# GeGLU feed-forward on one core: one plain feature tile instead of two, sixteen P2 tiles ahead instead of ten, and a new order of loads at the start

## The chip, the cores and the metric

The kernel runs on one core of one Trainium2 chip (trn2). The metric is the device time of one execution in microseconds (us). Executions of one kernel mostly agree within 0.3%, so differences of less than 1% have to be read with care here: every ratio below is that of a kernel to the kernel before, run in alternation with it on the same chip, and it comes with a 95% interval. Times in the text that begin "at 29.2 us" count from the start of the profiled span.

## The reference

```python
B, S, D, F = 32, 32, 1024, 3584          # 1024 tokens, bf16 throughout
def reference(x, w_gate, w_up, w_down):
    return (gelu_tanh(x @ w_gate) * (x @ w_up)) @ w_down
```

## The kernel before

The two projections x @ w_gate and x @ w_up are computed together, one 128-column feature tile at a time (28 tiles). For a tile, gate and up are the two block rows of a 2x2 block matrix A, the two halves of D are its block columns; x, transposed, is a 2x2 block matrix B of D halves by token halves. A plain product of the two costs 8 block products of 4 matmuls, 32 matmuls of 128x128 by 128x512. Twenty-six of the tiles are done with seven block products (Strassen-Winograd) instead, 28 matmuls: P1 = A11 B11, P2 = A12 B21, S1 T1, S2 T2, S3 T3, S4 B22 and A22 T4. P1 and P2 take bf16 operands as they come from memory; S1 to S4 (sums of weight blocks) and T1 to T4 (sums of x blocks) are made on chip in fp32r, a 4-byte type that the profile prints as f32 at the matmuls. Those tiles go in pairs ("chunks"). DVE makes the four T and the sums of the first pair, POOL makes the sums of all later pairs.

Products are summed up in banks of PSUM, the memory that PE writes; psA, psB and psC in the profile are such banks.

The first tiles are plain, because plain products need nothing but bf16 loads. Some P2 products also need only loads; they are made at the start and kept in fp32 ("ahead"), in groups of four tiles. So plain tiles and P2 groups are what TensorE (PE) does while x, the weights and the T matrices are still being prepared.

```python
FC = 2                       # tiles in a chunk
NAHEAD = 10                  # P2 tiles made ahead
KB = 4                       # P2 tiles in a group
...
# start of the queue of loads (SP); load_xT is a DMA transpose of x
load_ahead(0, 0, 1); ...                        # gate rows of group 0
load_xT(0, KD + KQ, DT)                         # rest of B21
load_ahead(0, KQ, KD)
load_w0(nc.sync, KD + KQ, DT)                   # weights of the plain tiles
load_ahead(1, 0, KD)
load_xT(0, 0, KD)                               # B11
load_w0(nc.sync, 0, KD)
load_xT(1, 0, KD)                               # B12
load_xT(1, KD, DT)                              # B22
... later: load_w_all(1, 1); load_w_all(1, 0)   # weights of the first pair
           load_ahead(2, 0, KD); load_w_all(2, 0)
...
# end of the start
tt(t2, b22, t1, SUB)
nc.scalar.copy(b22r, b22)
chunk1 = sums(1, nc.vector)                     # first pair's sums, on DVE
for _ in range(3):
    next(chunk1)
...
p1 = [acc("A") for _ in range(FC)]
for fl in range(FC):
    prod(p1[fl], quads(1, fl)[0], b11, True)    # P1 of the first pair
...
begun = [first_product(FC + fl, p1[fl]) for fl in range(FC)]   # adds ahead + P1 on DVE
tt(t3, b22, b12, SUB)
next(chunk1)
tt(t4, b21, t2, SUB)
nc.gpsimd.tensor_copy(ident[:, :1], t4[:, 0, :1])   # POOL starts only when T4 is there
...
for ci in range(1, NCH):                        # the pairs
    ... sums(ci + 1, nc.gpsimd)                 # next pair's sums, on POOL
    for fl in range(FC):
        prod(psc[fl], s1[fl], t1, True)
    for fl in range(FC):
        prod(psa[fl], s2[fl], t2, False)        # onto P1's bank: after DVE's add has read it
    for st in open_fts:
        last_product(st)                        # A22 T4 of the pair before
    ... S4 B22; P2, unless it was made ahead; P1 of the next pair; S3 T3
```

The down projection (w_down) follows as one more seven-product scheme; the change does not touch it.

Of the kernel before, what the change touches and what calls it, by code (L numbers as in the profile page):

```python
# [13 lines left out]
def kernel(  # L14
# [37 lines left out]
    NCH = FT // FC  # L52
    NAHEAD = 10
# [21 lines left out]

    def g_tiles(name, dtype, cols):

        return [
            gpool.tile(
                [P, k1 - k0, cols],  # L80
                dtype,
                name=name,
                tag=f"{name[:2]}{k1 - k0}",
                bufs=2,
            )
            for k0, k1 in batches
        ]

    g_lo = g_tiles("lo", bf16, N)
# [8 lines left out]
    def g_of(ft):  # L98
        k = ft % HF
        return by_batch(g_lo if ft < HF else g_hi)(k)  # L100
# [15 lines left out]
    def x_rows(dt, nb):  # L116
        return ((b11, b12), (b21, b22))[dt // KD][nb][:, dt % KD, :]


    ahead = [  # L120
        gpool.tile([P, n, NB], fp32, name="ahead", tag=f"hi{n}", bufs=2) for n in (KB, KB, QF - KB)
    ]
    assert 2 * KB < NAHEAD <= KB + QF
# [7 lines left out]
    def load_w(eng, ci, which, d0, d1):  # L131
        f0 = ci * FC * P
        src = (wg_r, wu_r)[which]
        eng.dma_start(out=w_tiles[ci, which][:, d0:d1, :], in_=src[:, d0:d1, f0 : f0 + FC * P])

    def load_w_all(ci, which):

        alloc_w(ci, which)
        if ci < NCH - 2:
            load_w(nc.sync, ci, which, 0, KD if which == 0 and is_ahead(ci) else DT)  # L140
            return


        for d0 in (0, KD):
            load_w(nc.sync, ci, which, d0, d0 + KD)

    def is_ahead(ci):
        return 0 < ci and (ci + 1) * FC <= FC + NAHEAD

    def quads(ci, fl=None):  # L150
        cols = slice(None) if fl is None else slice(fl * P, (fl + 1) * P)
        wg, wu = w_tiles[ci, 0], w_tiles[ci, 1]
        a12 = wg[:, KD:, cols]
        if is_ahead(ci):
            i, j = divmod((ci - 1) * FC, KB)
            a12 = a12_ahead[i][:, :, j * P : (j + FC) * P][:, :, cols]
# [4 lines left out]
    def sums(ci, eng):  # L161
# [3 lines left out]
            spool.tile([P, KD, FC * P], f32r, name=n, tag=n) for n in ("s1", "s2", "s4", "s3")  # L165
# [6 lines left out]

    a22rs = {}

    def a22r_of(ft):
        t = spool.tile([P, KD, P], f32r, name="a22r", tag="a22r", bufs=2)
        nc.scalar.copy(t, quads(*divmod(ft, FC))[3])
# [11 lines left out]
    with tc.manual_schedule():  # L189
# [12 lines left out]
        def load_ahead(i, k0, k1, eng=nc.sync):  # L202
            f0, n = FC + i * KB, min(KB, NAHEAD - i * KB)
            eng.dma_start(
                out=a12_ahead[i][:, k0:k1, : n * P],
                in_=wg_r[:, KD + k0 : KD + k1, f0 * P : (f0 + n) * P],
            )
# [14 lines left out]
        for which, eng in enumerate((nc.sync, nc.scalar)):  # L222
            load_w(eng, 0, which, KD, KD + KQ)
        load_xT(0, KD + KQ, DT)
# [4 lines left out]
        load_w0(nc.sync, 0, KD)  # L229
        load_xT(1, 0, KD)  # L230
        load_xT(1, KD, DT)

# [17 lines left out]
        def plain(ps, which, fl, nb, d0, d1, first=0, last=DT - 1):  # L250
            for dt in range(d0, d1):
                nc.tensor.matmul(  # L252
                    ps,
                    lhsT=w_tiles[0, which][:, dt, fl * P : (fl + 1) * P],
# [10 lines left out]
        def plain_out(ft, nb, h, up):  # L265
            tt(g_of(ft)[:, nb * NB : (nb + 1) * NB], h, up, MUL)
# [12 lines left out]
        def ahead_of(ft):  # L279
            i, j = divmod(ft - FC, KB)  # L280
            return ahead[i][:, j, :]

# [10 lines left out]


        ps = [acc(t) for t in "CCAA"]

        def plain0(tok0, d0, d1):
            for which in (0, 1):
                for dt in range(d0, d1):
                    for fl in range(FC):  # L300
                        plain(tok0[fl][which], which, fl, 0, dt, dt + 1, KD, KD - 1)
# [9 lines left out]
        tok0 = [(acc("A"), acc("B")) for _ in range(FC)]  # L311
        plain0(tok0, KD, KD + KQ)
        for j, copy in enumerate((nc.scalar.copy, nc.vector.tensor_copy) * 2):
            product_ahead(ps[j], 0, j, KQ)
            copy(ahead[0][:, j, :], ps[j])
        plain0(tok0, KD + KQ, DT)
        a12_ahead.append(xpool.tile([P, KD, (NAHEAD - 2 * KB) * P], bf16, name="a12b"))
        load_w_all(1, 1)
        load_w_all(1, 0)
        load_ahead(2, 0, KD)  # L320
        load_w_all(2, 0)
        for j, tag in enumerate("CCAA"):
            ps = acc(tag)
            product_ahead(ps, 1, j)
            (nc.scalar.copy, nc.vector.tensor_copy)[j % 2](ahead[1][:, j, :], ps)
        for fl in range(FC):
            for which in (0, 1):
                plain(tok0[fl][which], which, fl, 0, 0, KD, KD, KD - 1)
            plain_out(fl, 0, gelu(tok0[fl][0], "h0", 4), tok0[fl][1])
            if fl == 0:  # L330
                tt(t1, b12, b11, SUB)
        tok1 = [(acc("A"), acc("B")) for _ in range(FC)]
        for fl in range(FC):
            for which in (0, 1):
                plain(tok1[fl][which], which, fl, 1, 0, KD)
        tt(t2, b22, t1, SUB)
        nc.scalar.copy(b22r, b22)
# [3 lines left out]
        for fl in range(FC):  # L341
            for which in (0, 1):
                plain(tok1[fl][which], which, fl, 1, KD, DT)
            tok1[fl] = gelu(tok1[fl][0], "h0", 4), tok1[fl][1]
        load_w_all(2, 1)

# [11 lines left out]
        def first_product(ft, psa=None):  # L358
            if psa is None:
                psa = acc("A")  # L360
                prod(psa, quads(*divmod(ft, FC))[0], b11, True)
            if ft < FC + NAHEAD:
                return psa, gelu(added(ahead_of(ft), psa), "h0", 4)
# [252 lines left out]
```

## Time and profile before

| | before |
|---|---|
| time, median of 5 | 275.05 us (274.71 to 275.57) |
| profiled span | 273.3 us |
| PE busy | 267.9 us, 98% |
| first fp32r product (S1 T1 of the first pair) | at 29.18 us |
| S1 T1 of the second pair | at 38.36 us |
| a pair without / with its own P2 | 10.84 / 12.56 us |

The page's first part shows busy time, share of the span and number of instructions of each engine:

```profile
PE 267.9 (98%) x1190; PEld 188.9 (69%) x1206; DVE 196.6 (72%) x196; ACT 110.8 (41%) x181; POOL 108.3 (40%) x55
```

The list of waits, for PE alone (who waited, for what; us in total, times, longest), says that PE practically never waits:

```profile
PE psA L235 <- PEq L600: 0.8, 1, 0.8
PE psC L285 <- DMA a12a<-in_w_gate_dram: 0.5, 1, 0.5
```

PE's timeline around the first pair (start, duration, engine, line, operation; a merged row counts its matmuls, and its duration runs to the modelled end of the last one):

```profile
27.48 1.89 PE L285 MATMUL psC<-b,a12b 128*128 128x512 bf16 x8
29.18 2.12 PE L270 MATMUL psC<-t,s 128*128 128x512 f32 x8
31.13 2.00 PE L270 MATMUL psA<-t,s 128*128 128x512 f32 x8
32.97 1.98 PE L270 MATMUL psC<-b22r,s 128*128 128x512 f32 x8
36.33 2.19 PE L270 MATMUL psA<-t,s 128*128 128x512 f32 x8
38.36 1.98 PE L270 MATMUL psC<-t,s 128*128 128x512 f32 x8
```

Rows follow each other without a gap. From the starts of such rows, eight bf16 matmuls take 1.73 us (216 ns each) and eight fp32r ones 1.815 us (227 ns). The Trainium skill, "TensorE: Matmul & The Clock Gate", section Back-to-back issue gap, gives 512/2.4 + 2.5, about 216 ns, for the isolated spacing of matmuls with 512 columns; the bf16 rows agree with it, and the fp32r rows take 5% more.

DVE's timeline over the same stretch (first sum of the first pair, the two adds on P1's banks, T3, T4):

```profile
23.00 1.22 DVE L168 TENSOR_TENSOR s<-wu 128x1024 fp32r<-128x1024 bf16 x1
26.81 0.69 DVE L350 TENSOR_TENSOR c<-ahead,psA 128x512 f32<-128x512 f32 x1
27.68 0.69 DVE L350 TENSOR_TENSOR c<-ahead,psA 128x512 f32<-128x512 f32 x1 [0.17 <-PE psA L270]
28.28 2.28 DVE L379 TENSOR_TENSOR t<-b,b 128x2048 fp32r<-128x2048 bf16 x1
31.62 2.29 DVE L381 TENSOR_TENSOR t<-b,t 128x2048 fp32r<-128x2048 bf16 x1
```

The adds end at 28.4 us, and PE wants to accumulate S2 T2 onto those banks only at 31.13 us. T4 ends at 33.9 us; POOL then makes the second pair's S1, ready at 36.4 us, 1.9 us before PE wants it at 38.36. So DVE is busy, and has slack.

### The profile page before, as it was taken

The numbers are of one execution on the slowest core, as the hardware profiler recorded it, in microseconds if no ns is written. First come the engines' busy times: TensorE is split into PE (matmuls) and PEld (weight loads), VectorE is DVE, ScalarE is ACT, GpSimd is POOL, SyncE is SP. The second block draws the span as 40 slices with busy tenths as digits, with TensorE's granted clock in tenths as the row PEclk, the third lists the DMA queues.
The fourth block names the chain that finished last, engine by engine and source line by source line (L and its number), as shares of the span: only waits on it lengthen the run. The fifth ranks groups of instructions, "written<-read, shape, count | busy, mean of one in ns | idle before, by whom it ended". The sixth has DMA issues, their size and how long they took to land.

```text
span 273.3 us, 3350 instructions
## 1 busy us (share of the span) xinstructions
PE 267.9 (98%) x1190; PEld 188.9 (69%) x1206; DVE 196.6 (72%) x196; ACT 110.8 (41%) x181; POOL 108.3 (40%) x55
## 2 busy tenths in 40 slices
PE   8999999999999999999999999999999999999995
PEld 4444777877778676676868686754447888888883
DVE  1269996877756676776667576568999999999611
ACT  1271664554643646455563636430300032972001
POOL 1000099997897694949576684000000000000000
PEclk9999999999999999999999999999999999999999
DMA  7994321414505405050514280004992254786202
GB/s 166 290 251 105 111 75 40 117 42 113 156 11 143 137 19 155 0 153 0 156 28 126 79 269 1 0 2 132 329 342 83 93 175 163 240 279 203 78 0 78
DMA packets 53841, 33.77 MB, mean 124 GB/s; under 512 B 9792, under 2 KB 53824, under 8 KB 53824
## 3 DMA queue, kind: packets, MB, share of 16 engines
q1 hardware_dynamic: 50304, 31.00, 39.3%
q10 hardware_dynamic: 3520, 2.56, 2.9%
q8 instruction: 9, 0.15, 0.3%
q14 instruction: 8, 0.07, 0.1%
HBM read 29.62 MB, written 2.10 MB: 116 GB/s over the span
## 4 chain that ended last, share of the span: by engine, by line
PE 97%; DMA 1%; issue 0%; ACT 0%; SPq 0%
PE psA L270 34%; PE psA L446 18%; PE psC L270 17%; PE psC L446 7%; PE psB L446 7%; PE psB L270 5%; PE psB L252 3%; PE psA L252 2%; PE psC L285 2%; PE psA L285 1%; DMA a12a<-in_w_gate_dram 1%; ACT o_sb L586 0%; SPq L191 0%; PE tp L243 0%
## 5 line engine op out<-in xcount | busy, mean ns | idle before, releaser
L270 PE MATMUL psA<-t,s 128*128 128x512 f32 x208 | 54.2, 402 | 0.0
L262 ACT ACTIVATE h<-c 128x512 bf16<-128x512 f32 x52 | 31.6, 627 | 36.6 <-DVE c L350 36.6
L270 PEld LDWEIGHTS psA<-t,s 128*128 128x128 f32 x208 | 39.1, 188 | 9.2
L168 POOL TENSOR_TENSOR s<-wu 128x1024 fp32r<-128x1024 bf16 x12 | 27.4, 2285 | 23.7 <-PE psC L270 12.8
L350 DVE TENSOR_TENSOR c<-sn,psA 128x512 f32<-128x512 f32 x26 | 17.8, 684 | 16.8 <-PE psA L270 16.8
L270 PEld LDWEIGHTS <-wg 128*128 128x128 bf16 x168 | 15.4, 98 | 20.1 <-issue 3.4
L169 POOL TENSOR_TENSOR s<-s,wg 128x1024 fp32r<-128x1024 f32 x12 | 27.7, 2312 | 0.9
L171 POOL TENSOR_TENSOR s<-wg,wu 128x1024 fp32r<-128x1024 bf16 x12 | 26.6, 2216 | 0.0
L355 ACT COPY sn<-psA 128x512 f32<-128x512 f32 x42 | 23.6, 584 | 6.8 <-PE psA L270 6.8
L355 ACT COPY sn<-psC 128x512 f32<-128x512 f32 x26 | 15.2, 588 | 26.9 <-PE psC L270 22.8
L270 PE MATMUL psA<-t,a22r 128*128 128x512 f32 x104 | 25.9, 391 | 0.0
L270 PE MATMUL psC<-t,s 128*128 128x512 f32 x104 | 25.8, 390 | 0.0
L270 PE MATMUL psC<-b22r,s 128*128 128x512 f32 x104 | 25.7, 389 | 0.0
L270 PE MATMUL psA<-b,wg 128*128 128x512 bf16 x100 | 24.1, 379 | 0.2
L270 PEld LDWEIGHTS psC<-t,s 128*128 128x128 f32 x104 | 19.4, 188 | 4.4 <-ACT ahead L377 0.3
L270 PEld LDWEIGHTS psA<-t,a22r 128*128 128x128 f32 x104 | 19.5, 188 | 4.1
L270 PEld LDWEIGHTS psC<-b22r,s 128*128 128x128 f32 x104 | 19.5, 188 | 4.1
L350 DVE TENSOR_TENSOR c<-sn,psC 128x512 f32<-128x512 f32 x26 | 17.7, 688 | 5.5 <-PE psC L270 5.5
L369 DVE TENSOR_TENSOR hi<-h,psA 128x512 bf16<-128x512 bf16 x14 | 9.6, 689 | 12.5 <-PE psA L270 12.5
L425 DVE TENSOR_TENSOR hi<-c,h 128x512 bf16<-128x512 f32 x14 | 18.0, 1284 | 0.5
L425 DVE TENSOR_TENSOR lo<-c,h 128x512 bf16<-128x512 f32 x12 | 17.8, 1479 | 0.6
L170 POOL TENSOR_TENSOR s<-wg,s 128x1024 fp32r<-128x1024 bf16 x8 | 17.3, 2156 | 0.6
(94 smaller groups left out, 396.9 us busy)
## 6 DMA issues: line engine op xcount, KB each, us to landing
wdb<-in_w_down_dram SPq DMA_DIRECT2D x12, 512.0 KB, 5.0
wu<-in_w_up_dram SPq DMA_DIRECT2D x11, 512.0 KB, 4.0
wdb<-in_w_down_dram SPq DMA_DIRECT2D x12, 384.0 KB, 4.7
wg<-in_w_gate_dram SPq DMA_DIRECT2D x6, 512.0 KB, 5.1
wg<-in_w_gate_dram SPq DMA_DIRECT2D x10, 256.0 KB, 4.4
v<-in_w_down_dram SPq DMA_DIRECT2D x4, 512.0 KB, 6.7
out_dram<-o_sb ACTq DMA_DIRECT2D x16, 128.0 KB, 1.7
v<-in_w_down_dram SPq DMA_DIRECT2D x4, 384.0 KB, 7.6
```

The lines of the kernel that those rows point to most:

```text
L168: yield eng.tensor_tensor(s1, a21, a22, ADD)
L169: yield eng.tensor_tensor(s2, s1, a11, SUB)
L170: yield eng.tensor_tensor(s4, a12, s2, SUB)
L171: yield eng.tensor_tensor(s3, a11, a21, SUB)
L252: nc.tensor.matmul(ps, lhsT=w_tiles[0, which][:, dt, fl * P : (fl + 1) * P], rhs=x_rows(dt, nb), start=(dt == first), stop=(dt == last),)
L262: nc.scalar.activation(h, src, ACT.Gelu_apprx_tanh)
L270: nc.tensor.matmul(ps, lhsT=lhs[:, k, :], rhs=rhs[:, k, :], start=(start and k == 0), stop=(k == KD - 1), skip_group_check=True,)
L350: tt(t, s, ps, ADD)
L355: nc.scalar.copy(t, ps)
L369: tt(g_of(ft)[:, :NB], h0, psa, MUL)
L425: tt(g_of(ft)[:, NB:], added(sn5[fl], psa[fl]), h1[fl], MUL)
L446: nc.tensor.matmul(banks[m], lhsT=lhs(k)[:, m * P : (m + 1) * P], rhs=rhs(k), start=(start and k == 0), stop=(k == HF - 1), skip_group_che ...
```

## The change

Its intent is to do one more tile with 28 matmuls instead of 32, and to fill the gap that the missing plain tile leaves with P2 products made ahead (16 tiles instead of 10, four groups). One tile is then left over and forms the last "pair". In the queue of loads the third gate group goes ahead of the x of the other tokens (B12, B22), and the fourth behind it, ahead of the first pair's weights. T3 goes ahead of the two adds on P1's banks. The core of the diff (cuts marked; the bookkeeping of buffers is left out):

```diff
-    NAHEAD = 10
+    chunks = [range(0, 1)] + [range(f0, min(f0 + FC, FT)) for f0 in range(1, FT, FC)]
+    NCH = len(chunks)
+    NAHEAD = 16
 ...
         load_ahead(1, 0, KD)
         load_xT(0, 0, KD)
         load_w0(nc.sync, 0, KD)
+        load_ahead(2, 0, KD)
         load_xT(1, 0, KD)
         load_xT(1, KD, DT)
+        load_ahead(3, 0, KD)
+        for which in (1, 0):
+            load_w_all(1, which)
+        load_w_all(2, 0)
 ...
-        for fl in range(FC):                       # two plain tiles
-            for which in (0, 1):
-                plain(tok0[fl][which], which, fl, 0, 0, KD, KD, KD - 1)
-            plain_out(fl, 0, gelu(tok0[fl][0], "h0", 4), tok0[fl][1])
+        group_ahead(1, "CCAA", both)
+        for which in (0, 1):
+            plain(tok0[which], which, 0, 0, KD, KD, KD - 1)
+        plain_out(0, gelu(tok0[0], "h0", 4), tok0[1])
+        group_ahead(2, "CCAA")
+        tt(t1, b12, b11, SUB)
 ... (plain products of the other tokens, T2, three sums)
+        tt(t3, b22, b12, SUB)
+        load_w_all(2, 1)
+        group_ahead(3, "CCAA")
+        nc.scalar.copy(b22r, b22)
 ... (P1 of the first pair, its adds)
-        tt(t3, b22, b12, SUB)
         next(chunk1)
         tt(t4, b21, t2, SUB)
```

Below, "group 3" and "group 4" are the third and fourth gate group (indices 2 and 3 in the code), as in the prediction.

More of the change, by code (lines that the diff above doesn't have):

```diff
@@ L51 @@
     FC = 2
-    NCH = FT // FC
-    NAHEAD = 10
+    chunks = [range(0, 1)] + [range(f0, min(f0 + FC, FT)) for f0 in range(1, FT, FC)]
+    NCH = len(chunks)
+    NAHEAD = 16
     KQ = DT // 4
@@ L74, with g_tile @@
     ps1 = ctx.enter_context(tc.tile_pool(name="ps1", bufs=2, space=bass.MemoryType.PSUM))
+    def g_tile(name, b, dtype=bf16, cols=N):
+        k0, k1 = batches[b]
+        return gpool.tile([P, k1 - k0, cols], dtype, name=name, tag=f"{name[:2]}{k1 - k0}", bufs=2)
     def g_tiles(name, dtype, cols):
-        return [
-            gpool.tile(
-                [P, k1 - k0, cols],
-                dtype,
-                name=name,
-                tag=f"{name[:2]}{k1 - k0}",
-                bufs=2,
-            )
-            for k0, k1 in batches
-        ]
-    g_lo = g_tiles("lo", bf16, N)
+        return [g_tile(name, b, dtype, cols) for b in range(len(batches))]
+    ahead = [gpool.tile([P, KB, NB], fp32, name="ahead", tag=f"lo{KB}", bufs=2)]
+    g_lo = [g_tile("lo", b) for b in range(2)]
+    g_hi = []
     def by_batch(tiles):
@@ L98, in g_of @@
     def g_of(ft):
-        k = ft % HF
-        return by_batch(g_lo if ft < HF else g_hi)(k)
+        k, name, tiles = ft % HF, ("lo", "hi")[ft // HF], (g_lo, g_hi)[ft // HF]
+        if k in (k0 for k0, _ in batches[len(tiles) :]):
+            tiles.append(g_tile(name, len(tiles)))
+        return by_batch(tiles)(k)
     BANKS = {"A": 4, "B": 2, "C": 2}
@@ L117, in x_rows @@
         return ((b11, b12), (b21, b22))[dt // KD][nb][:, dt % KD, :]
-    ahead = [
-        gpool.tile([P, n, NB], fp32, name="ahead", tag=f"hi{n}", bufs=2) for n in (KB, KB, QF - KB)
-    ]
-    assert 2 * KB < NAHEAD <= KB + QF
+    ahead += [gpool.tile([P, n, NB], fp32, name="ahead", tag=f"hi{n}", bufs=2) for n in (KB, QF - KB) * 2]
+    ahead_at = [t[:, k, :] for t in ahead for k in range(t.shape[1])]
+    assert NAHEAD <= len(ahead_at) and NAHEAD % KB == 0
     w_tiles = {}
@@ L131, in load_w @@
     def load_w(eng, ci, which, d0, d1):
-        f0 = ci * FC * P
+        f0, n = chunks[ci][0] * P, len(chunks[ci]) * P
         src = (wg_r, wu_r)[which]
-        eng.dma_start(out=w_tiles[ci, which][:, d0:d1, :], in_=src[:, d0:d1, f0 : f0 + FC * P])
+        eng.dma_start(out=w_tiles[ci, which][:, d0:d1, :n], in_=src[:, d0:d1, f0 : f0 + n])
     def load_w_all(ci, which):
         alloc_w(ci, which)
-        if ci < NCH - 2:
-            load_w(nc.sync, ci, which, 0, KD if which == 0 and is_ahead(ci) else DT)
+        if (ci, which) != (NCH - 1, 0):
+            load_w(nc.sync, ci, which, 0, KD if which == 0 and a12_stays(ci) else DT)
             return
@@ L145, in load_w_all, with a12_stays @@
             load_w(nc.sync, ci, which, d0, d0 + KD)
-    def is_ahead(ci):
-        return 0 < ci and (ci + 1) * FC <= FC + NAHEAD
+    def a12_stays(ci):
+        return 1 <= chunks[ci][0] and chunks[ci][-1] < 1 + 2 * KB
     def quads(ci, fl=None):
-        cols = slice(None) if fl is None else slice(fl * P, (fl + 1) * P)
+        cols = slice(0, len(chunks[ci]) * P) if fl is None else slice(fl * P, (fl + 1) * P)
         wg, wu = w_tiles[ci, 0], w_tiles[ci, 1]
         a12 = wg[:, KD:, cols]
-        if is_ahead(ci):
-            i, j = divmod((ci - 1) * FC, KB)
+        if a12_stays(ci):
+            i, j = divmod(chunks[ci][0] - 1, KB)
             a12 = a12_ahead[i][:, :, j * P : (j + FC) * P][:, :, cols]
@@ L164, in sums @@
         s1, s2, s4, s3 = (
-            spool.tile([P, KD, FC * P], f32r, name=n, tag=n) for n in ("s1", "s2", "s4", "s3")
+            spool.tile([P, KD, FC * P], f32r, name=n, tag=n)[:, :, : len(chunks[ci]) * P]
+            for n in ("s1", "s2", "s4", "s3")
         )
@@ L171, in sums, with chunk_of @@
         yield eng.tensor_tensor(s3, a11, a21, SUB)
+    def chunk_of(ft):
+        ci = next(i for i, c in enumerate(chunks) if ft in c)
+        return ci, ft - chunks[ci][0]
     a22rs = {}
@@ L176, in a22r_of @@
         t = spool.tile([P, KD, P], f32r, name="a22r", tag="a22r", bufs=2)
-        nc.scalar.copy(t, quads(*divmod(ft, FC))[3])
+        nc.scalar.copy(t, quads(*chunk_of(ft))[3])
         a22rs[ft] = t
@@ L202, in load_ahead @@
         def load_ahead(i, k0, k1, eng=nc.sync):
-            f0, n = FC + i * KB, min(KB, NAHEAD - i * KB)
+            f0 = 1 + i * KB
             eng.dma_start(
-                out=a12_ahead[i][:, k0:k1, : n * P],
-                in_=wg_r[:, KD + k0 : KD + k1, f0 * P : (f0 + n) * P],
+                out=a12_ahead[i][:, k0:k1, :],
+                in_=wg_r[:, KD + k0 : KD + k1, f0 * P : (f0 + KB) * P],
             )
@@ L223 @@
             load_w(eng, 0, which, KD, KD + KQ)
+        a12_ahead += [spool.tile([P, KD, KB * P], bf16, name="a12b", tag=t) for t in ("s2", "s4")]
         load_xT(0, KD + KQ, DT)
@@ L248, with plain @@
         transposed(0)
-        def plain(ps, which, fl, nb, d0, d1, first=0, last=DT - 1):
+        def plain(ps, which, nb, d0, d1, first=0, last=DT - 1):
             for dt in range(d0, d1):
@@ L253, in plain @@
                     ps,
-                    lhsT=w_tiles[0, which][:, dt, fl * P : (fl + 1) * P],
+                    lhsT=w_tiles[0, which][:, dt, :P],
                     rhs=x_rows(dt, nb),
@@ L263, in gelu, with plain_out @@
             return h
-        def plain_out(ft, nb, h, up):
-            tt(g_of(ft)[:, nb * NB : (nb + 1) * NB], h, up, MUL)
+        def plain_out(nb, h, up):
+            tt(g_of(0)[:, nb * NB : (nb + 1) * NB], h, up, MUL)
         def prod(ps, lhs, rhs, start):
@@ L277, in prod @@
                 )
-        def ahead_of(ft):
-            i, j = divmod(ft - FC, KB)
-            return ahead[i][:, j, :]
         def product_ahead(ps, i, j, k0=0, k1=KD, cols=slice(None)):
@@ L292, in product_ahead, with group_ahead @@
                 )
-        ps = [acc(t) for t in "CCAA"]
-        def plain0(tok0, d0, d1):
-            for which in (0, 1):
-                for dt in range(d0, d1):
-                    for fl in range(FC):
-                        plain(tok0[fl][which], which, fl, 0, dt, dt + 1, KD, KD - 1)
+        def group_ahead(i, tags, copies=(nc.scalar.copy,)):
+            for j, tag in enumerate(tags):
+                ps = acc(tag)
+                product_ahead(ps, i, j)
+                copies[j % len(copies)](ahead_at[i * KB + j], ps)
+        ps = [acc(t) for t in "CCAA"]
         for k in range(KQ):
@@ L310 @@
                     transposed(1)
-        tok0 = [(acc("A"), acc("B")) for _ in range(FC)]
-        plain0(tok0, KD, KD + KQ)
-        for j, copy in enumerate((nc.scalar.copy, nc.vector.tensor_copy) * 2):
-            product_ahead(ps[j], 0, j, KQ)
-            copy(ahead[0][:, j, :], ps[j])
-        plain0(tok0, KD + KQ, DT)
-        a12_ahead.append(xpool.tile([P, KD, (NAHEAD - 2 * KB) * P], bf16, name="a12b"))
-        load_w_all(1, 1)
-        load_w_all(1, 0)
-        load_ahead(2, 0, KD)
-        load_w_all(2, 0)
-        for j, tag in enumerate("CCAA"):
-            ps = acc(tag)
-            product_ahead(ps, 1, j)
-            (nc.scalar.copy, nc.vector.tensor_copy)[j % 2](ahead[1][:, j, :], ps)
-        for fl in range(FC):
-            for which in (0, 1):
-                plain(tok0[fl][which], which, fl, 0, 0, KD, KD, KD - 1)
-            plain_out(fl, 0, gelu(tok0[fl][0], "h0", 4), tok0[fl][1])
-            if fl == 0:
-                tt(t1, b12, b11, SUB)
-        tok1 = [(acc("A"), acc("B")) for _ in range(FC)]
-        for fl in range(FC):
-            for which in (0, 1):
-                plain(tok1[fl][which], which, fl, 1, 0, KD)
+        both = (nc.scalar.copy, nc.vector.tensor_copy)
+        tok0 = (acc("A"), acc("B"))
+        for which in (0, 1):
+            plain(tok0[which], which, 0, KD, KD + KQ, KD, KD - 1)
+        for j in range(KB):
+            product_ahead(ps[j], 0, j, KQ)
+            both[j % 2](ahead_at[j], ps[j])
+        for which in (0, 1):
+            plain(tok0[which], which, 0, KD + KQ, DT, KD, KD - 1)
+        group_ahead(1, "CCAA", both)
+        for which in (0, 1):
+            plain(tok0[which], which, 0, 0, KD, KD, KD - 1)
+        plain_out(0, gelu(tok0[0], "h0", 4), tok0[1])
+        group_ahead(2, "CCAA")
+        tt(t1, b12, b11, SUB)
+        tok1 = (acc("A"), acc("B"))
+        for d0 in (0, KD):
+            for which in (0, 1):
+                plain(tok1[which], which, 1, d0, d0 + KD)
+        tok1 = gelu(tok1[0], "h0", 4), tok1[1]
         tt(t2, b22, t1, SUB)
-        nc.scalar.copy(b22r, b22)
         chunk1 = sums(1, nc.vector)
@@ L340 @@
             next(chunk1)
-        for fl in range(FC):
-            for which in (0, 1):
-                plain(tok1[fl][which], which, fl, 1, KD, DT)
-            tok1[fl] = gelu(tok1[fl][0], "h0", 4), tok1[fl][1]
+        tt(t3, b22, b12, SUB)
         load_w_all(2, 1)
+        group_ahead(3, "CCAA")
+        nc.scalar.copy(b22r, b22)
         def added(s, ps):
@@ L360, in first_product @@
                 psa = acc("A")
-                prod(psa, quads(*divmod(ft, FC))[0], b11, True)
-            if ft < FC + NAHEAD:
-                return psa, gelu(added(ahead_of(ft), psa), "h0", 4)
+                prod(psa, quads(*chunk_of(ft))[0], b11, True)
+            if ft <= NAHEAD:
+                return psa, gelu(added(ahead_at[ft - 1], psa), "h0", 4)
             return psa, snap(psa, "sn1")
@@ L373 @@
             prod(p1[fl], quads(1, fl)[0], b11, True)
-        for j, tag in enumerate("CC"):
-            ps = acc(tag)
-            product_ahead(ps, 2, j)
-            nc.scalar.copy(ahead[2][:, j, :], ps)
-        begun = [first_product(FC + fl, p1[fl]) for fl in range(FC)]
-        tt(t3, b22, b12, SUB)
+        begun = [first_product(ft, p1[fl]) for fl, ft in enumerate(chunks[1])]
         next(chunk1)
@@ L383 @@
         nc.gpsimd.tensor_copy(ident[:, :1], t4[:, 0, :1])
-        for fl in range(FC):
-            plain_out(fl, 1, *tok1[fl])
+        plain_out(1, *tok1)
         open_fts = []
         for ci in range(1, NCH):
-            fts = range(ci * FC, (ci + 1) * FC)
-            if fts[0] == HF:
-                g_hi = g_tiles("hi", bf16, N)
+            fts = chunks[ci]
             if ci + 1 < NCH:
@@ L395 @@
                     pass
-            s1, s2, s3, s4 = ([s[:, :, fl * P : (fl + 1) * P] for fl in range(FC)] for s in s_tiles[ci])
+            s1, s2, s3, s4 = ([s[:, :, fl * P : (fl + 1) * P] for fl in range(len(fts))] for s in s_tiles[ci])
             sn5, sn2, h1, h0 = [], [], [], []
@@ L399 @@
             psc = [acc("C") for _ in fts]
-            for fl in range(FC):
+            for fl in range(len(fts)):
                 prod(psc[fl], s1[fl], t1, True)
                 sn5.append(snap(psc[fl], "sn5"))
-            for fl in range(FC):
+            for fl in range(len(fts)):
                 prod(psa[fl], s2[fl], t2, False)
@@ L413 @@
                 load_w_all(ci + 2, 1)
-            if fts[0] < FC + NAHEAD:
+            if fts[-1] <= NAHEAD:
                 h0 = first
             else:
-                for fl in range(FC):
+                for fl in range(len(fts)):
                     psb = acc("B")
@@ L421 @@
                     h0.append(gelu(added(first[fl], psb), "h0", 4))
-            begun = [first_product(ft + FC) for ft in fts] if ci + 1 < NCH else []
+            begun = [first_product(ft) for ft in chunks[ci + 1]] if ci + 1 < NCH else []
             for fl, ft in enumerate(fts):
```

## The prediction

> **What bounds it now.** The matmul stream. The page gives PE 98% busy (267.9 of 273.3 us); the chain of waits is 97% PE; PE's list of waits has two entries (0.8 us for the start, 0.5 us for the first gate rows). In PE's timeline eight bf16 matmuls of 512 columns take 1.73 us (216 ns each), eight fp32r ones 1.815 us (227 ns). The Trainium skill ("TensorE: Matmul & The Clock Gate", Back-to-back issue gap) gives about 216 ns as isolated spacing: the bf16 rows agree, the fp32r rows are 5% slower. A pair of tiles without its own P2 takes 10.84 us against 40 x 227 + 8 x 216 = 10.80; one with P2 12.56 against 12.53. So no stage hides a stall; only fewer or cheaper matmuls, or new stalls, move the time.
>
> **What changes on PE.** One feature tile goes from plain (32 bf16 matmuls, 6.91 us) to seven products (28: 8 bf16, 20 fp32r, 1.73 + 4.54 = 6.27 us). Gain: 0.64 us, 0.23%, all on the critical path. Sixteen P2 tiles ahead instead of 10 move 24 matmuls from loop to start at the same price. The single last tile has less cover for its waits, but those (a snap of 0.6 us, an add of 0.7 us) fit under the pair's two last products and the P2.
>
> **What it adds off PE.** From the first product at 4.45 us, the start shrinks from 112 to 104 full-size matmuls (24.2 to 22.4 us): the first seven-product pair begins near 27.5 us instead of 29.2, while more must have arrived. Packets in the trace take 18, 27 and 46 ns (medians for 256, 512, 1024 bytes): tile 0's weights keep their packet count at half the size, saving about 1.1 us of the 16 DMA engines; each extra gate group costs about 1.6 us. Landings estimated from the before trace, against need:
> - second part of the first gate group: 7.5, 7.6 us
> - last weights of tile 0: 13.2, 13.7
> - gate group 3: 14.9, 15.4
> - x of the other tokens: 16.4 and 18.6, 18.9 and 20.6
> - group 4: 21, 22.3
> - first pair's weights: 22.5 and 23.5; DVE wants them at 22, PE at 25.8
>
> It fits, with margins of 0.1 to 2 us. DVE is the other tight chain: T1, T2, three sums, T3 (2.28 us, now ahead), then P1's two adds, ending near 29.2 and 29.8 us; PE accumulates on those banks at 29.3 and 30.2. T4 ends near 33.3; then POOL makes the second pair's sums, the first ready near 35.7 against 36.7. Slack was 2 us, now about 1. Later POOL needs 9.2 us a pair against a 10.84 us period, so eight P2-free pairs instead of five don't starve PE.
>
> **Prediction.** 275.05 - 0.64 = 274.4 us if everything fits; with 0.2 us for small stalls at the start 274.6 us, 8 in 10 between 273.9 and 275.8. Faster by over 2%: 1%; within 2%: 97%; slower: 2%.
>
> **What would show it.** Right: PE busy about 0.6 us lower, PE's waits under 2 us, periods 10.84 and 12.56 us unchanged, first fp32r product near 27.5 us. Wrong: PE waits on gate or x landings between 7.6 and 22 us, on DVE's adds between 29 and 31 us, on POOL's sums at the second pair, or at the last tile.
>
> **What would make it wrong.** Gate group 3 delaying x and the first pair's weights more than estimated: DVE's chain shifts whole, and PE stalls as much at P1's banks and the second pair, perhaps 1 to 2 us, cancelling the gain.

## The result, and the profile after

| | before | after |
|---|---|---|
| time, median of 5 | 275.05 us | 278.38 us (fast ones 278.10 to 278.52) |
| ratio, after to before | | 1.0116 (1.0100 to 1.0132) |
| taken again in a second series, 5 rounds | 275.07 us | 278.08 us, ratio 1.0113 (1.0094 to 1.0132) |

Ratios are computed as the mean time of one kernel's fast runs over that of the other's of the same rounds, so they are not quite the ratio of the medians quoted beside them. The change costs 1.1%, about 3.1 us. The predicted 274.6 us and the range up to 275.8 us were wrong, and so was the direction; that the change would stay within 2% was right.

One of the five executions, the profiled one, took 1576.64 us. It counts as slow (over 1.5% above the fastest of its kernel) and is not used: in it PE was busy for 1570.8 us and the mean fp32r matmul took 1.7 us. No other execution of any kernel here did this, and no run explains it. The profile used for the changed kernel is therefore that of the second series (span 276.2 us). Its list of PE's waits:

```profile
PE psC L293 <- DMA a12b<-in_w_gate_dram: 1.8, 2, 0.9
PE psA L282 <- DVE c L351: 1.1, 1, 1.1
PE psA L247 <- PEq L593: 0.8, 1, 0.8
PE psC L293 <- DMA a12a<-in_w_gate_dram: 0.5, 1, 0.5
```

Two waits for gate groups (a12b holds groups 3 and 4) and one for DVE's adds are new. PE's timeline shows where they stand:

```profile
16.45 1.90 PE L293 MATMUL psC<-b,a12b 128*128 128x512 bf16 x8 [0.90 <-DMA a12b<-in_w_gate_dram]
24.41 1.90 PE L293 MATMUL psC<-b,a12b 128*128 128x512 bf16 x8 [0.88 <-DMA a12b<-in_w_gate_dram]
29.42 2.20 PE L282 MATMUL psC<-t,s 128*128 128x512 f32 x8
32.68 2.12 PE L282 MATMUL psA<-t,s 128*128 128x512 f32 x8 [1.06 <-DVE c L351]
38.00 2.19 PE L282 MATMUL psA<-t,s 128*128 128x512 f32 x8
40.02 1.98 PE L282 MATMUL psC<-t,s 128*128 128x512 f32 x8
```

The first pair starts at 29.42 us, not at the predicted 27.5, and it lasts 10.60 us (29.42 to 40.02) against 9.18 before: PE stood before S2 T2. From 40.02 us on, nothing is lost: pairs take 10.83 and 12.56 us as before. DVE's timeline shows what came late:

```profile
18.37 2.29 DVE L333 TENSOR_TENSOR t<-b,b 128x2048 fp32r<-128x2048 bf16 x1 [2.02 <-DMA b<-in_x_dram]
26.08 1.23 DVE L170 TENSOR_TENSOR s<-wu 128x1024 fp32r<-128x1024 bf16 x1 [3.09 <-DMA wu<-in_w_up_dram]
29.74 2.28 DVE L343 TENSOR_TENSOR t<-b,b 128x2048 fp32r<-128x2048 bf16 x1
31.94 1.28 DVE L351 TENSOR_TENSOR c<-ahead,psA 128x512 f32<-128x512 f32 x2
34.27 2.28 DVE L377 TENSOR_TENSOR t<-b,t 128x2048 fp32r<-128x2048 bf16 x1
```

DVE waits 3.09 us for the first pair's up weights and starts its sums at 26.08 us, where it had started at 23.00. T3 then stands between the sums and the adds; the adds end at 33.2 us.

The landings, from the time at which SP issued each load and its time to landing, against the prediction's estimates:

| load | estimated | measured after | wanted |
|---|---|---|---|
| second part of the first gate group | 7.5 | 7.48 | 7.6 |
| last weights of tile 0 | 13.2 | 13.37 | 13.7 |
| gate group 3 | 14.9 | 16.40 | 15.4 |
| x of the other tokens, B12 and B22 | 16.4, 18.6 | 18.35, 20.35 | 18.9, 20.6 |
| gate group 4 | 21 | 24.37 | 22.3 |
| first pair's weights, up and gate | 22.5, 23.5 | 26.06, 26.95 | 22, 25.8 |

The estimates hold as far as 13.4 us. Then there are two jumps, 1.5 us at group 3 and another 1.6 us at group 4, and everything behind keeps them. (Two other profiles with this order of loads, the slow execution and the kernel with T3 behind the adds, have the up weights at 25.33 and 25.78 us: a landing varies by 0.7 us from one execution to the next.)

### The profile page after: what moved, and what is told of

The parts are those of the page before. It is cut to its first block, busy times and chain, and to the rows that moved or that the text cites. A ratio compares the mean times of both kernels' runs of the same rounds, so it can differ in the third digit from the quotient of the medians.

```text
span 1574.8 us, 3375 instructions
## 1 busy us (share of the span) xinstructions
PE 1570.8 (100%) x1202; PEld 869.8 (55%) x1202; DVE 198.3 (13%) x199; ACT 119.4 (8%) x185; POOL 107.5 (7%) x59
## 4 chain that ended last, share of the span: by engine, by line
PE 100%; ACT 0%; issue 0%
PE psA L282 36%; PE psA L439 19%; PE psC L282 18%; PE psB L439 7%; PE psC L439 7%; PE psB L282 4%; PE psC L293 3%; PE psA L293 3%; PE psA L264 1%; PE psB L264 1%; PE psA L247 1%; PE tp L255 0%; ACT o_sb L579 0%
## 5 line engine op out<-in xcount | busy, mean ns | idle before, releaser
L282 PE MATMUL psA<-t,s 128*128 128x512 f32 x216 | 310.4, 1770 | 0.0
L282 PEld LDWEIGHTS psA<-t,s 128*128 128x128 f32 x216 | 198.3, 918 | 95.9 <-issue 88.9
L282 PE MATMUL psC<-t,s 128*128 128x512 f32 x108 | 148.8, 1715 | 0.0
L282 PE MATMUL psA<-t,a22r 128*128 128x512 f32 x108 | 148.6, 1700 | 0.0
L282 PE MATMUL psA<-b,wg 128*128 128x512 bf16 x108 | 147.8, 1708 | 0.0
L282 PE MATMUL psC<-b22r,s 128*128 128x512 f32 x108 | 147.6, 1680 | 0.0
L282 PEld LDWEIGHTS psC<-t,s 128*128 128x128 f32 x108 | 99.2, 919 | 44.3 <-issue 44.3
L282 PEld LDWEIGHTS psA<-t,a22r 128*128 128x128 f32 x108 | 98.4, 911 | 45.0 <-issue 45.0
L282 PEld LDWEIGHTS psC<-b22r,s 128*128 128x128 f32 x108 | 97.7, 904 | 45.2 <-issue 45.2
L439 PE MATMUL psA<-v,hi 128*128 128x512 bf16 x56 | 74.4, 1708 | 0.0
```

The source lines that it names most:

```text
L282: nc.tensor.matmul(ps, lhsT=lhs[:, k, :], rhs=rhs[:, k, :], start=(start and k == 0), stop=(k == KD - 1), skip_group_check=True,)
L439: nc.tensor.matmul(banks[m], lhsT=lhs(k)[:, m * P : (m + 1) * P], rhs=rhs(k), start=(start and k == 0), stop=(k == HF - 1), skip_group_che ...
```

## The experiments

The theories:

- **A: the loads.** The two extra groups make everything behind them land late; the second plain tile, which would have covered that, is gone. PE waits for the groups; DVE's chain (sums, T3, adds, T4) begins late, and POOL with it.
- **B: the order of T3 and the adds** is a cost of its own.
- **C: the loop or the single last tile** loses time. The second profile ended this one: pairs are unchanged from 40 us on.

All experiments but one are edits of the changed kernel. Each kernel's profile is one execution, and executions of the kernels with late loads spread by 0.4 to 2.8 us, so a landing or a wait of a few tenths may be that execution's own.

### The changed kernel again

No edit.

> The changed kernel unaltered, because its recorded profile fell in an execution in which every matmul took about 1.7 us (1575 us in all), which tells nothing of the 278.4 us of the others. Expected: 278.1 to 278.6 us again. Theory A (the start: late gate group, x or first weights, then DVE's chain): the PE timeline shows 3.5 to 4.5 us of gaps before 45 us and none later, with pairs at 10.84 and 12.56 us. Theory B (the single last tile): gaps of about that size between the last pair and the down projection. Theory C (the loop: POOL or DMA cannot keep up with eight P2-free pairs): pairs longer than 10.84 us after 45 us.

Measured: 278.08 us, ratio 1.0113. The gaps are all before 45 us, as under theory A; that is the profile shown above.

### Without the load of group 4, of group 3, of both

These kernels give a wrong result: products of a group that is not loaded read the rows of an earlier group. PE's, DVE's, ACT's and POOL's work stays the same.

```diff
-        load_ahead(2, 0, KD)      # group 3
-        load_ahead(3, 0, KD)      # group 4
-                    lhsT=a12_ahead[i][:, k, j * P : (j + 1) * P],
+                    lhsT=a12_ahead[i - 2 if i in (2, 3) else i][:, k, j * P : (j + 1) * P],
```

Without group 4:

> Wrong on purpose: the last ahead group (tiles 13 to 16) is not loaded; its products read the rows of the second group instead. PE's work is unchanged. Theory A (the extra loads make the start late: x, group 4, the first pair's weights, and through them DVE's chain): the first pair's up weights land near 23 us instead of 26.05, the wait for group 4 (0.9 us) and the stall at P1's banks (1.1 to 1.4 us) go, only group 3's 0.9 us stays: 275.8 us, 275.4 to 276.3. Theory B (the order of T3 and the adds): the stall stays, about 277.2 us.

Without group 3:

> Wrong on purpose: group 3 (tiles 9 to 12), which the change loads ahead of the x of the other tokens, is not loaded; its products read the first group's rows. Theory A: x, group 4 and the weights land 2.5 to 3.5 us earlier than in the changed kernel; all three waits go or shrink under 0.3 us: 274.7 us, 274.3 to 275.2. If it is rather the sum of both groups that matters and the transposes gain little, 275.5 to 276.5. Theory B: near 277 us.

Without both:

> Wrong on purpose: neither group is loaded; both read the rows of the first two. The changed kernel's whole instruction stream on PE, DVE, ACT and POOL, without its extra loads. Theory A: no stall is left, and the arithmetic of the prediction shows: 274.4 us, 274.1 to 274.8. Theory B: 275.5 us or more.

Without both, once more:

> The kernel without the two extra loads once more (wrong on purpose, unaltered), to measure the bare gain: the prediction's arithmetic says ratio 0.9977 (0.64 us less), the first five rounds gave 0.9992 (0.9979 to 1.0005). If the arithmetic holds, 0.9970 to 0.9983; if some 0.3 us of it is lost elsewhere, 0.9985 to 0.9995.

| kernel | median | before, same rounds | ratio (95%) | up weights landed |
|---|---|---|---|---|
| changed | 278.08 us | 275.07 us | 1.0113 (1.0094 to 1.0132) | 26.06 us |
| without group 4 | 276.51 us | 275.37 us | 1.0038 (1.0024 to 1.0053) | 26.96 us, see below |
| without group 3 | 276.31 us | 275.37 us | 1.0034 (1.0020 to 1.0048) | 24.60 us |
| without both | 275.07 us | 275.37 us | 0.9992 (0.9979 to 1.0005) | 22.65 us |
| without both, again | 275.11 us | 275.11 us | 1.0003 (0.9989 to 1.0017) | 22.57 us |

Without the two loads the loss is gone. In the last profile PE waits for nothing but the two things that it waited for before:

```profile
PE psA L245 <- PEq L591: 0.8, 1, 0.8
PE psC L291 <- DMA a12a<-in_w_gate_dram: 0.6, 1, 0.6
```

and its first pair starts at 27.51 us, as predicted for a start without stalls, and runs through:

```profile
27.51 2.19 PE L280 MATMUL psC<-t,s 128*128 128x512 f32 x8
29.54 1.98 PE L280 MATMUL psA<-t,s 128*128 128x512 f32 x8
```

In the first series, DVE starts the first pair's sums, when the up weights have landed, at 22.68 us:

```profile
22.68 1.23 DVE L170 TENSOR_TENSOR s<-wu 128x1024 fp32r<-128x1024 bf16 x1 [1.40 <-DMA wu<-in_w_up_dram]
```

Its second pair starts at 36.75 us (40.02 in the changed kernel), and its span is 273.0 us against 276.2: 3.27 us of difference at the second pair, 3.2 at the end. So the loads are the whole of the loss. T3 stands ahead of the adds in this kernel too and costs nothing there, so theory B by itself is out.

Two things did not come as expected. First, leaving out one group alone left 0.7 and 1.6 us more than theory A expected (276.5 for 275.8, 276.3 for 274.7; for group 3 this is the alternative named beforehand, that the sum of both groups matters): the up weights still land at 24.60 us without group 3 (in its slowest execution), and DVE's adds still hold PE for 0.9 us. The profile of the kernel without group 4 fell in its second slowest execution (278.94 us, median 276.51), in which all loads of the start were late; its landings are not typical. Second, the bare gain of the arithmetic, 0.64 us (ratio 0.9977), did not show. The two series give 0.9992 and 1.0003, the intervals of both leave out 0.9977, and 275.07 us lies outside the expected 274.1 to 274.8. In the traces, the last row of 56 products starts at 256.83 us in the second series of this kernel and at 257.29 us before, 0.46 us earlier: about 0.06 us is lost in the first pair (9.24 for 9.18 us), as much again over the loop with its single last tile, and as much at the start. The rest of the difference, some 0.3 us, is not resolved.

### T3 behind the adds

```diff
-        tt(t3, b22, b12, SUB)
 ...
         begun = [first_product(ft, p1[fl]) for fl, ft in enumerate(chunks[1])]
+        tt(t3, b22, b12, SUB)
```

> T3 goes back behind P1's two adds, the rest of the change stays. Theory B (T3 ahead of the adds is a cost of its own): the stall at P1's banks goes and nothing comes in its place: 276.7 to 277.1 us. Theory A (DVE's whole chain from the landing of the first pair's weights to T4 is late, and POOL starts only at T4's end): the stall at P1's banks goes but returns as a wait for POOL's first two sums at the second pair: 277.7 us, 277.4 to 278.1.

Measured: 277.66 us, ratio 1.0089 (1.0066 to 1.0111). The stall at P1's banks is gone, and a new one stands at the second pair, where POOL's first sum is not ready:

```profile
PE psC L282 <- POOL s L170: 0.5, 1, 0.5
```

The second pair then also lasts 11.39 us instead of 10.83: the loading of its S2 weights waits for POOL's second sum, which PE's own list does not show. With the first pair at 9.90 us (9.24 without the loads) the pairs lose 1.22 us, against 1.36 in the changed kernel. This is what theory A expected: the whole chain on DVE is late (T4 ends at 36.3 us, 36.6 in the changed kernel), and which instruction PE meets first is a matter of order. The ratios differ by some 0.7 us, but the intervals of the two kernels overlap, so a cost of T3's place is not shown. In this profile the two group waits were also shorter (0.4 us each), so part of the 0.7 us is the landings of that execution.

### The same two loads in the kernel before

To the kernel before, with its two plain tiles, two loads of the same size were added at the same places; nobody reads them, and the result is correct.

```diff
+        spare = [spool.tile([P, KD, KB * P], bf16, name="spare", tag=t) for t in ("s2", "s4")]
+        load_spare(0)             # 512 KB of gate rows
         load_xT(1, 0, KD)
         load_xT(1, KD, DT)
+        load_spare(1)
```

> The kernel before, with two plain tiles and its own P2 tiles, plus two loads of 512 KB of gate rows that nobody reads: one ahead of the x of the other tokens, one behind it, where the changed kernel has its groups 3 and 4. Theory A with cover (the loads delay the first pair's weights by about 4 us, but the second plain tile's matmuls cover most of it): weights land near 26 us, first pair at 29.2 us as before, T4 ends near 37 us, and PE waits about 1 to 1.5 us for POOL's first sums at the second pair: 276.3 us, ratio 1.002 to 1.006. If the cover of the second plain tile does not matter and the loads alone are the loss, about 278.3 us as in the changed kernel. If loads nobody waits for cost nothing, 275.1 us.

Measured: 277.09 us, ratio 1.0064 (1.0043 to 1.0085). The landings are those of the changed kernel almost to the tenth: B12 at 18.35, B22 at 20.43, the up weights at 26.14 us (18.35, 20.35, 26.06 there). With the second plain tile as cover, that costs 1.8 us (0.64% of 275.27) instead of 3.1. PE's list has one new wait, where P1 wants the gate weights:

```profile
PE psA L278 <- DMA wg<-in_w_gate_dram: 1.1, 1, 1.1
```

So the loads alone cost 1.8 us even with the old cover. That the other 1.3 us of the change are the cover that was taken away is the plain reading, but no run takes the cover away alone. The expected 276.3 us was too low: the wait came for the gate weights, which I had not counted. Of the expected wait for POOL's sums a remnant is there: the second pair lasts 11.08 us instead of 10.83, its S2 weights waiting for POOL's second sum.

### The loads in another order

Four orders of the same bytes. The first keeps all transposes together:

```diff
         load_ahead(1, 0, KD)
-        load_xT(0, 0, KD)
         load_w0(nc.sync, 0, KD)
         load_ahead(2, 0, KD)
+        load_xT(0, 0, KD)
         load_xT(1, 0, KD)
         load_xT(1, KD, DT)
         load_ahead(3, 0, KD)
```

(PE makes group 3 before tile 0's last products; DVE makes T1 before tile 0's output.)

> The changed kernel with the same loads in another order: tile 0's last weights and gate group 3 go ahead of all the remaining transposes of x, so that no ordinary load stands between two transposes; PE makes group 3 before tile 0's last products. If ordinary loads between transposes cost time by themselves (the transposes' first packets sit until the loads ahead have drained), x, group 4 and the weights land about 1 us earlier, the wait for group 3 goes: 277.3 us. If only the sum of bytes matters, they land as late as before, and just the wait for group 3 goes: 277.8 us or more.

Measured: 277.13 us, ratio 1.0066 (1.0049 to 1.0083). Group 3 now lands at 12.56 us and PE does not wait for it; group 4 lands at 22.78 us and the up weights at 24.44 us, 1.6 us earlier than in the changed kernel, with the same bytes ahead of them. PE still waits 0.4 us for group 4 and 1.0 us for DVE's adds. This points to where the two jumps in the landings come from. It shows in the distance from one landing to the next: here group 3 lands 1.52 us after the load ahead of it (11.04 to 12.56); in the changed kernel it lands 3.03 us after (13.37 to 16.40) and 4.4 us after the transpose before those. Behind the last transpose it is much the same in every kernel. The view of the loads (size, time from issue to landing) has group 4 and the up weights of the changed kernel, issued at 18.06 and 18.68 us, as:

```profile
a12b<-in_w_gate_dram SPq DMA_DIRECT2D x1, 512.0 KB, 6.3
wu<-in_w_up_dram SPq DMA_DIRECT2D x1, 512.0 KB, 7.4
```

and the first load behind the last transpose in the kernel before, the up weights, issued at 16.42 us:

```profile
wu<-in_w_up_dram SPq DMA_DIRECT2D x1, 512.0 KB, 5.5
```

B22 had landed at 20.35 us; group 4 needs 4.0 us more, the weights behind it 1.7 us. In the kernel before, B22 landed at 18.67 and the weights at 21.87 us, 3.2 us later. Over the thirteen profiles of the kernel before, the changed one and the experiments, the first 512 KB behind the last transpose landed 2.8 to 4.8 us after it, and the next 512 KB, where there is one, 1.6 to 1.9 us after that. By these figures a return from transposes to ordinary loads takes, as an estimate, some 1 to 3 us on top of the bytes. The changed kernel has two returns behind B11 and B22, and this order takes one away; but the kernel before has these two as well, and the kernel without the extra loads too, so returns are not what the change added.

How far the order itself helps is not settled. This profile is that of the fastest of six executions (276.44 us; median 277.13), and the next order, which also keeps the transposes together, has its up weights at 26.01 us, in its slowest execution.

The packets in the trace show a part of what happens, at the change into transposes rather than out of them. A 256-byte packet takes 18 ns as a rule. When the transpose of B12 begins behind group 3 in the changed kernel, 17 such packets take 0.87 to 1.30 us each, and all end between 16.22 and 16.27 us, when SP is through with issuing that transpose (16.25) and just before group 3 has landed. Their sum is 1.2 us of all 16 DMA engines. In the kernel before it is 15 packets of 0.16 to 0.40 us at this place, 0.24 us of the engines; here, with the transposes together, 0.23 us; in the profile of the next order, 1.6 us. Behind the last transpose the queue is then less busy for about 1 us (before: 122 and 169 GB/s from 18.0 to 19.0 us, 292 GB/s at 17.0 and 340 at 20.0). What the engines wait for there, the records do not show. SP is a rival cause of late landings: issuing the transposes of B11, B12 and B22 takes it 10.3 us in the changed kernel (9.2 before), and the up weights' load is issued only at 18.68 us (16.42 before). Against that, without both loads it was issued at 16.00 and 16.32 us, earlier than before, and landed later (22.65 and 22.57 us against 21.87). No run tests it alone.

The second order puts both gate groups ahead of the remaining x, with T3 behind the adds (the moved lines of PE's and DVE's work are left out here and in the next two):

```diff
         load_ahead(1, 0, KD)
-        load_xT(0, 0, KD)
         load_w0(nc.sync, 0, KD)
         load_ahead(2, 0, KD)
+        load_ahead(3, 0, KD)
+        load_xT(0, 0, KD)
         load_xT(1, 0, KD)
         load_xT(1, KD, DT)
-        load_ahead(3, 0, KD)
```

> The changed kernel with both extra gate groups ahead of the remaining x, PE makes groups 2 to 4 in a row, T3 behind the adds. PE then never waits for a landing before the second pair (x at 19.5 to 22 us against a need at 20.6 to 24.5), but the first pair's weights still land near 25 us, so T4 ends near 35.5 us and PE waits for POOL at the second pair about 1.7 us: 276.2 us, 275.7 to 276.8. If the waits of PE for landings were the whole loss, 274.7 us.

Measured: 276.56 us, ratio 1.0044 (1.0027 to 1.0061). In its profile (the slowest of its six executions) no landing of x or of groups 3 and 4 holds PE, but the up weights land at 26.01 us, T4 ends at 36.5 us, and PE waits for POOL at the second pair:

```profile
PE psC L282 <- POOL s L170: 1.1, 1, 1.1
```

The second pair again lasts 11.39 us, so POOL costs 1.7 us in all, as expected. Earlier, PE waits 0.81 us for the second gate group.

The third loads the first pair's weights ahead of group 4, with P1 before group 4 on PE and T3 behind the adds:

```diff
+        for which in (1, 0):
+            load_w_all(1, which)
         load_ahead(3, 0, KD)
-        for which in (1, 0):
-            load_w_all(1, which)
         load_w_all(2, 0)
```

> The changed kernel with the first pair's weights loaded ahead of gate group 4 and PE making P1 of the first pair before group 4, T3 behind the adds. Same bytes. Theory A: the weights land near 23.6 and 24.5 us, DVE's chain ends at 34.5 us, no wait for POOL; PE waits about 1 us for P1's weights and group 3's 0.9 us stays: 276.8 us, 276.3 to 277.3.

Measured: 278.28 us, ratio 1.0113 (1.0096 to 1.0130), no gain at all, against 276.8 expected. The weights landed at 25.0 and 25.9 us, 1.4 us later than I had counted on (again the return from the transposes, 3.8 us, and x itself 0.9 us later than in the changed kernel's profile); PE waited 1.4 us for P1's weights, and its first fp32r product began at 30.93 us. The wait had only changed its place.

The last takes the first pair's weights ahead of the transposes as well, lets DVE make all four sums of that pair while x is still on its way, puts T3 behind the adds, and gives PE group 4 after S1 T1:

```diff
         load_ahead(1, 0, KD)
-        load_xT(0, 0, KD)
         load_w0(nc.sync, 0, KD)
         load_ahead(2, 0, KD)
+        for which in (1, 0):
+            load_w_all(1, which)
+        load_xT(0, 0, KD)
         load_xT(1, 0, KD)
         load_xT(1, KD, DT)
         load_ahead(3, 0, KD)
-        for which in (1, 0):
-            load_w_all(1, which)
         load_w_all(2, 0)
 ... 
+        for _ in sums(1, nc.vector):
+            pass
         tt(t1, b12, b11, SUB)
 ...
+            if ci == 1:
+                group_ahead(3, "BBBB")
```

> The changed kernel's work with all ordinary loads but the last gate group ahead of the remaining x: tile 0's last weights, group 3 and the first pair's weights, then the three transposes, then group 4. DVE makes the first pair's four sums while x is still on its way, PE makes the pair's first product with T1 before group 4. If DVE's chain behind late weights and the change from transposes to ordinary loads were the loss: weights land near 15 us, T4 ends near 31 us, x lands at 17, 19 and 21 us (PE waits 0.3 us at most), group 4 near 25 us, before it is needed: 275.2 us, 274.8 to 275.6, level with the kernel before within what can be told. If something else holds the changed kernel back, 276.5 us or more.

Measured: 276.12 us, ratio 1.0041 (1.0028 to 1.0053), between the two expectations. DVE's chain is out of the way: T4 ends at 31.4 us instead of 36.6, DVE even idles 2.5 us behind it, and neither DVE nor POOL holds PE. What is left is x itself, which now lands at 20.05 and 22.08 us:

```profile
PE psA L264 <- DMA b<-in_x_dram: 0.8, 1, 0.8
```

This is 2 us better than the change as it was made, and no correct version did better (both gate groups first, 1.0044, is too close to tell apart); it is still 0.4% slower than the kernel before.

## Why the prediction was wrong, point by point

- **What bounds the kernel before: right.** Matmuls follow each other at 216 and 227 ns, and PE's list of waits is empty but for the start.
- **The gain on PE, 0.64 us: right in kind, too large in size.** Without the extra loads the first pair starts at 27.51 us, as predicted (27.5), and the last row of products starts 0.46 us earlier than before; in the measured times no gain is clear of the noise (ratios 1.0003 and 0.9992, and both intervals leave out the predicted 0.9977). The prediction's own sign, "PE busy about 0.6 us lower", did not come either: 267.9 us before and after, 268.2 without the loads. It could not decide, because the traces lack some matmul records (1190 matmuls beside 1206 weight loads before, 1185 beside 1202 after).
- **"Landings estimated from the before trace": wrong; this is the step that failed.** Group 3 was put at 14.9 us and landed at 16.40; x at 16.4 and 18.6, measured 18.35 and 20.35; group 4 at 21, measured 24.37; the first pair's weights at 22.5 and 23.5, measured 26.06 and 26.95. For the up weights the estimate can be taken apart: read from the running sum of bytes in the before trace they land at 20.3 us; less the 1.1 us saved on tile 0's weights, plus two groups of 1.6 us, that is 22.4, the 22.5 of the list but for rounding. The first two terms were wrong. The profile's own landing before is 21.87 us, 1.6 us later than the sum says. And the saving did not show: without the two loads the same weights landed at 22.65 and 22.57 us, 0.7 us later than before instead of 1.1 earlier. These two make up 3.4 of the 3.6 us that are missing.
- **"Each extra gate group costs about 1.6 us": about right for what comes behind it.** From without both to the changed kernel the up weights move by 3.4 us, 1.7 us a group (in the kernel before, by 4.3 us with the two unused loads; single executions all). It is the group's own landing that was too early: a group that follows other ordinary loads takes 1.4 to 1.9 us, but the first 512 KB behind the last transpose landed 2.8 to 4.8 us after it, and group 3, with two loads of 128 KB between it and a transpose and another transpose behind it, took 1.9 to 3.0 us. The trace of before already showed it: its up weights landed 3.2 us after B22. I had overlooked it because I read landings from the running sum of bytes. The Trainium skill, "DMA: Bandwidth & Descriptors", section Why a DMA increments its semaphore by 16 and not by 1, says that a DMA runs on up to 16 engines that finish independently, and that each engine's signal "lands only after that engine's data"; so a load has landed when its slowest engine is done, and bytes of later loads on faster engines count in the sum before that. The before trace agrees: when the up weights landed, at 21.87 us, the sum stood some 500 KB beyond their end.
- **The margins of 0.1 to 2 us: they were the warning.** The prediction named its own failure ("Gate group 3 delaying x and the first pair's weights more than estimated ... perhaps 1 to 2 us") and gave it too little weight. The delay of the weights was 3.5 us, and PE's stalls sum to 0.90 + 0.88 us for the groups and 1.36 us in the first pair (10.60 for 9.24 us), 3.1 us, which is the measured loss against the kernel without the loads (3.2 us).
- **DVE's adds near 29.2 and 29.8 us: wrong, as a consequence.** They ended at 33.2 us. The chain itself was reckoned rightly: without the loads, where the up weights landed at 22.57 us, the adds ended at 29.7 and T4 at 33.1 us (predicted 29.8 and 33.3). T3's new place is not a cause of its own: with the weights on time it costs nothing.
- **POOL and DVE in the loop, the single last tile: right. POOL at the second pair: right in part by luck.** Pairs keep 10.83 and 12.56 us, and PE does not wait there. But in the changed kernel POOL's first sum is ready only at 39.1 us, and PE escapes it because it is late itself (40.02 us); where T3 stood behind the adds, it did wait. Without the loads the sum is ready at 35.6 us against 36.75, as predicted (35.7 against 36.7).

What stays open: why loads next to transposes land so late and so unevenly (the records do not tell the DMA engines apart), why half the bytes for tile 0 brought the later loads forward by next to nothing (B22 at 18.54 us for 18.67), some 0.3 us of the bare gain, and the one execution of 1577 us.

## What to carry to other kernels

At the start of a tuned kernel the matmuls are not only work but cover for the loads, so count, for each piece that is moved there, matmul time per byte loaded: the plain tile gave 6.9 us of matmuls for 0.5 MB, a P2 group gives 3.5 us for the same 0.5 MB, and exchanging one for the other made a start that was fed just in time starve. Take landings from each load's own issue and landing, never from bytes summed over all of them, and treat a margin smaller than the error of that reading as a stall. Where an estimate moves many landings at once, check first where they stand without the change: here that base was off by 3.4 us, and the cost of the added loads by 0.2. Where loads of two kinds share a queue, try keeping each kind together; three orders that did so lost 0.4 to 0.7% instead of 1.1%, though no run tells how much of that is the order of kinds and how much the order of needs.

## What the Trainium skill lacked or had wrong

- "DMA: Bandwidth & Descriptors", Rules for kernel authors, says "A transpose next to ordinary DMAs needs nothing". That holds for correctness in every run here that was not wrong on purpose, but it says nothing of time: the first 512 KB ordinary load behind the last DMA transpose landed 2.8 to 4.8 us after it (thirteen profiles), while the next 512 KB, where there was one, took 1.6 to 1.9 us more; and where a transpose began behind a 512 KB load, 17 packets that take 18 ns as a rule took up to 1.30 us.
- "TensorE: Matmul & The Clock Gate", Back-to-back issue gap, gives its spacings without regard to the operands' type. Here 512-column bf16 matmuls keep 216 ns, and fp32r matmuls, whose weight loads take 188 ns instead of 98 ns, keep 227 ns. The section also gives 131 ns as the sustained rate for 512 columns; no row of these traces keeps it.
- The same page, section Seeing it yourself, tells of a clock gate seen stuck for 50 us and more. One execution here was slow from end to end: 1576.64 us, with eight bf16 matmuls in 10.6 us where 1.73 is usual. I found no page that has that, and the profile has no clock row for it, so whether it is the same thing is not shown.
